# Setting the bulk elementwise work of neighbouring chunks between the two operations of a scan step

## The chip, the cores and the metric

The kernel runs on one core of a Trainium2 chip. The time is device time in microseconds (us) of one execution. A run more than 1.5% above the fastest of its kernel counts as slow. Medians below are of all runs, ratios of the fast runs alone. Comments in the cuts of code and of diffs are added here.

## The reference

A gated linear-attention layer is followed by a mixture of experts that sends each row to one expert. Only the attention part matters here, above all its decay `a`, whose modulus is cut at 0.999, and the running product over time.

```python
mag = np.sqrt(a_re * a_re + a_im * a_im)
scale = np.minimum(mag, 0.999) / (mag + 1e-06)
a_re_n, a_im_n = (a_re * scale, a_im * scale)
for t in range(S):                      # S = 768
    ar, ai = (a_re_n[:, :, t, :, None], a_im_n[:, :, t, :, None])
    new_re = ar * S_re - ai * S_im
    new_im = ar * S_im + ai * S_re
    ...                                 # kv, the product of k and v of this step
    S_re, S_im = (new_re + kv, new_im)
    y[:, :, t] = np.einsum('bhd,bhde->bhe', q[:, :, t], S_re)
```

## The kernel before

The sequence is cut into pieces of L = 96 steps. `elem(r)` treats half of all pieces (a round), one in each of 128 partitions. It runs a scan of complex products backwards over the 96 steps: each step is a multiply into `x` and an add into `A[:, t]`, and the add of one step feeds the multiply of the next. The round is worked in 12 chunks of T = 8 steps. Around the scan stands bulk work on whole chunks: the modulus stage, which makes the normalised `a` (`an`), and the stage that turns the finished scan into scaled q (`Qh`) and k. Then `units(r)` does the matmuls of the round. The program order is `elem(0)`, `units(0)`, `elem(1)`, `units(1)`, experts. A scheduler places the instructions of all stages into the queues of the engines, so part of `elem(1)` runs beside `units(0)`.

```python
st = ctx.enter_context(tc.tile_pool(name="st", bufs=2))
...
def elem(r):
    A = qt.tile([P, L + 1, 2, D], F32, name="A")
    QT = qt.tile([C, P, L], F32, name="QT")          # one buffer each
    ...
    for c in range(L // T - 1, -1, -1):
        t0 = c * T
        ...                                           # load ab
        sq = st.tile([P, 2, T, D], F32, name="sq")
        nc.scalar.activation(sq[:], ab[:], Act.Square)
        m = st.tile([P, T, D], F32, name="m", bufs=3)
        nc.vector.tensor_tensor(m[:], sq[:, 0], sq[:, 1], Alu.add)
        ...                                           # Ln, Exp, Copy on ScalarE: m, g
        nc.vector.scalar_tensor_tensor(g[:], m[:], 1.0, g[:], Alu.min, Alu.mult)
        an = st.tile([P, T, 4, D], F32, name="an")
        nc.vector.tensor_tensor(an[...], ab[:], planes(g, T), Alu.mult)
        ...                                           # two copies of an on ScalarE
        for t in range(t0 + T - 1, t0 - 1, -1):       # the scan
            x = st.tile([P, 2, 2, D], F32, name="x")
            nc.vector.tensor_tensor(x[:], A[:, t + 1, ...], an[:, t - t0]..., Alu.mult)
            nc.vector.tensor_tensor(A[:, t], x[:, 0], x[:, 1], Alu.add)
        ...                                           # load qc, kc
        e = A[:, t0 + 1:t0 + T + 1]
        sq = st.tile([P, T, 2, D], F32, name="sqe", tag="sq")      # shares the ring of sq
        nc.scalar.activation(sq[:], e, Act.Square)
        m = st.tile([P, T, D], F32, name="me", tag="m", bufs=3)    # shares the ring of m
        nc.vector.tensor_tensor(m[:], sq[:, :, 0], sq[:, :, 1], Alu.add)
        ...                                           # Ln, Exp on ScalarE
        nc.vector.tensor_tensor(qc[:], qc[:], m[:], Alu.mult)
        nc.vector.tensor_tensor(Qh[:], e, qc..., Alu.mult)
        nc.vector.tensor_tensor(e, e, kc..., Alu.mult)
        ...                                           # store e, transpose Qh on PE, copy to QT
```

Of the kernel before, what the change touches and what calls it, by code (L numbers as in the profile page):

```python
# [10 lines left out]
F32 = mybir.dt.float32  # L11
BF16 = mybir.dt.bfloat16
AX = mybir.AxisListType
Alu = mybir.AluOpType
Act = mybir.ActivationFunctionType
# [7 lines left out]
def gate_loop(nc, ctx, tc, cpool, ident, identb, q, k, v, a_re, a_im, wgp, x_rows, lg):  # L23


    B, H, S, D = q.shape
    L = 96
    G = S // L
    P = 128
# [3 lines left out]
    C = 2 * D  # L33
    T = 8

    qt = ctx.enter_context(tc.tile_pool(name="qt", bufs=1))
    st = ctx.enter_context(tc.tile_pool(name="st", bufs=2))
    un = ctx.enter_context(tc.tile_pool(name="un", bufs=2))
    ps = ctx.enter_context(tc.psum_pool(name="aps", bufs=1))

    kh = nc.dram_tensor("kh", (NR, P, L, C), F32, kind="Internal").ap()
# [6 lines left out]
    def rows(x, r):  # L48
        return x[r * NB:(r + 1) * NB].rearrange("b h (g t) d -> (b h g) t d", t=L)

    def planes(x, n):
        return x[:, None].broadcast_to([P, 2, n, D])

    for_round = []

    def elem(r):
        A = qt.tile([P, L + 1, 2, D], F32, name="A")
        QT = qt.tile([C, P, L], F32, name="QT")
        for_round.append(QT)
        nc.vector.memset(A[:, L, 0, :], 1.0)  # L60
        nc.vector.memset(A[:, L, 1, :], 0.0)
        for c in range(L // T - 1, -1, -1):
            t0 = c * T
            ab = st.tile([P, 2, T, D], F32, name="ab")
            nc.sync.dma_start(out=ab[:, 0], in_=rows(a_re, r)[:, t0:t0 + T])
            nc.sync.dma_start(out=ab[:, 1], in_=rows(a_im, r)[:, t0:t0 + T])
            sq = st.tile([P, 2, T, D], F32, name="sq")
            nc.scalar.activation(sq[:], ab[:], Act.Square)
            m = st.tile([P, T, D], F32, name="m", bufs=3)
            nc.vector.tensor_tensor(m[:], sq[:, 0], sq[:, 1], Alu.add)  # L70

            nc.scalar.activation(m[:], m[:], Act.Ln, scale=1.0 / (0.999 * 0.999))
            nc.scalar.activation(m[:], m[:], Act.Exp, scale=-0.5)
            g = st.tile([P, T, D], F32, name="g")
            nc.scalar.activation(g[:], m[:], Act.Copy, scale=-1e-6 / 0.999, bias=1.0)  # L75
            nc.vector.scalar_tensor_tensor(g[:], m[:], 1.0, g[:], Alu.min, Alu.mult)

            an = st.tile([P, T, 4, D], F32, name="an")
            nc.vector.tensor_tensor(an[:, :, 0:2, :].rearrange("p t c d -> p c t d"), ab[:], planes(g, T), Alu.mult)
            nc.scalar.activation(an[:, :, 2, :], an[:, :, 1, :], Act.Copy, scale=-1.0)  # L80
            nc.scalar.activation(an[:, :, 3, :], an[:, :, 0, :], Act.Copy)  # L81
            for t in range(t0 + T - 1, t0 - 1, -1):
                x = st.tile([P, 2, 2, D], F32, name="x")
                nc.vector.tensor_tensor(x[:], A[:, t + 1, :, None, :].broadcast_to([P, 2, 2, D]), an[:, t - t0].rearrange("p (u w) d -> p u w d", u=2), Alu.mult)  # L84
                nc.vector.tensor_tensor(A[:, t], x[:, 0], x[:, 1], Alu.add)  # L85

            qc = st.tile([P, T, D], F32, name="qc")
            kc = st.tile([P, T, D], F32, name="kc")
            nc.sync.dma_start(out=qc[:], in_=rows(q, r)[:, t0:t0 + T])
            nc.sync.dma_start(out=kc[:], in_=rows(k, r)[:, t0:t0 + T])  # L90
            e = A[:, t0 + 1:t0 + T + 1]
            sq = st.tile([P, T, 2, D], F32, name="sqe", tag="sq")
            nc.scalar.activation(sq[:], e, Act.Square)  # L93
            m = st.tile([P, T, D], F32, name="me", tag="m", bufs=3)
            nc.vector.tensor_tensor(m[:], sq[:, :, 0], sq[:, :, 1], Alu.add)
            nc.scalar.activation(m[:], m[:], Act.Ln)
            nc.scalar.activation(m[:], m[:], Act.Exp, scale=-1.0)
            nc.vector.tensor_tensor(qc[:], qc[:], m[:], Alu.mult)
            Qh = st.tile([P, T, 2, D], F32, name="Qh")
            nc.vector.tensor_tensor(Qh[:], e, qc[:, :, None, :].broadcast_to([P, T, 2, D]), Alu.mult)  # L100
            nc.vector.tensor_tensor(e, e, kc[:, :, None, :].broadcast_to([P, T, 2, D]), Alu.mult)
            nc.sync.dma_start(out=kh[r, :, t0:t0 + T], in_=e.rearrange("p t c d -> p t (c d)"))
            for t4 in range(0, T, 4):
                tp = ps.tile([C, 4, P], F32, name="tq", tag="tp", bufs=2)
                for i in range(4):
                    nc.tensor.transpose(tp[:, i, :], Qh[:, t4 + i].rearrange("p c d -> p (c d)"), ident[:])  # L106
                nc.scalar.copy(QT[:, :, t0 + t4:t0 + t4 + 4], tp.rearrange("c t p -> c p t"))
        nc.sync.dma_start(out=c_scr[r], in_=A[:, 0].rearrange("p c d -> p (c d)"))

    def units(r):  # L110
# [77 lines left out]

    nc.scalar.preload_act_table_set("natural_log_exp_and_others")
    elem(0)  # L190
    for r in range(NR):
        units(r)
        if r + 1 < NR:
            elem(r + 1)
# [184 lines left out]
def kernel(  # L379
# [34 lines left out]
    with ExitStack() as gstack:  # L414
        gate_loop(nc, gstack, tc, cpool, ident, identb, q, k, v, a_re, a_im, wgp, x_rows, lg)
# [31 lines left out]
```

## Time and profile before

| | before |
|---|---|
| median of the runs | 916.6 us at first; 909.96 us of the four runs that stand against the changed kernel |
| first scan stage, from the first multiply to the last bulk multiply | 147.7 us |
| first units stage, to its last mask multiply | 153.3 us |
| the rest of `elem(1)`, with no matmuls of units beside it ("scan alone") | 100.9 us |
| second units stage, to the first weight load | 155.3 us |
| the rest: weights and experts | 351.2 us |

A stage is read from the start times in the timeline of VectorE. In a timeline line stand the start, the duration, the engine, the source line, the operation, out and in, and in brackets the idle time just before it and what ended it. In the kernel before, the square of the finished chunk (L93) comes first, and the square of the next chunk's `a` (L68) only behind it, although its input was there long before (the loads were issued at 10.6 and 10.9 us, and no load of `ab` took over 5.3 us):

```profile
28.73 0.84 ACT L93 ACTIVATE sqe<-A 128x768 f32<-128x768 f32 x1 [4.82 <-DVE A L85]
29.48 0.83 ACT L68 ACTIVATE sq<-ab 128x768 f32<-128x768 f32 x1
...
35.44 0.52 ACT L80 ACTIVATE an<-an 128x384 f32<-128x384 f32 x1
35.87 0.51 ACT L81 ACTIVATE an<-an 128x384 f32<-128x384 f32 x1
```

ScalarE sat idle for 4.82 us before L93, while VectorE ran the scan, and the L68 behind it, which was ready, did not pass it. The copies L80 and L81, for which the next scan waits, end only at 36.38 us. VectorE kept its order in the same way: the scan multiply at 215.71 us (0.34 us) had its result at 216.05, but the add that reads it started only at 216.97, behind a `state` operation (L169) for which the engine sat idle for 0.65 us until 216.69.

### The profile page before, as it was taken

The numbers are of one execution on the slowest core, as the hardware profiler recorded it, in microseconds if no ns is written. First come the engines' busy times: TensorE is split into PE (matmuls) and PEld (weight loads), VectorE is DVE, ScalarE is ACT, GpSimd is POOL, SyncE is SP. The second block draws the span as 40 slices with busy tenths as digits, with TensorE's granted clock in tenths as the row PEclk, the third lists the DMA queues.
The fourth block names the chain that finished last, engine by engine and source line by source line (L and its number), as shares of the span: only waits on it lengthen the run. The fifth ranks groups of instructions, "written<-read, shape, count | busy, mean of one in ns | idle before, by whom it ended". The sixth has DMA issues, their size and how long they took to land. (4 is left out here: it accounts for less than half of the span.)

```text
span 919.8 us, 11601 instructions
## 1 busy us (share of the span) xinstructions
PE 586.6 (64%) x3599; PEld 373.8 (41%) x3599; DVE 375.7 (41%) x835; ACT 281.5 (31%) x620; POOL 82.6 (9%) x122
## 2 busy tenths in 40 slices
PE   0111111798899811117999995008999999999996
PEld 0011111566667611115667774006444444444443
DVE  5777777127657777770243331160111111111100
ACT  4444454134545745532233432000111111111111
POOL 0000000000000000000000002212222121221201
PEclk9999999997868965555578968555656666665657
DMA  4233333424543243214233313996010110101100
GB/s 120 88 103 103 103 97 87 100 66 99 134 115 85 65 155 103 80 34 101 66 88 78 88 44 44 207 208 123 26 40 31 35 39 27 40 28 38 23 1 1
DMA packets 104774, 71.58 MB, mean 78 GB/s; under 512 B 72878, under 2 KB 96930, under 8 KB 104720
## 3 DMA queue, kind: packets, MB, share of 16 engines
q0 software_dynamic: 14992, 20.36, 10.9%
q1 hardware_dynamic: 24768, 30.82, 10.8%
q10 hardware_dynamic: 64960, 19.67, 9.7%
q8 instruction: 35, 0.57, 0.3%
q14 instruction: 19, 0.16, 0.1%
HBM read 66.79 MB, written 17.99 MB: 92 GB/s over the span
## 5 line engine op out<-in xcount | busy, mean ns | idle before, releaser
L364 PE MATMUL h_ps<-xgT,w1s 128*128 128x128 bf16 x744 | 169.1, 248 | 20.6 <-DVE xgT L357 14.6
L106 PE MATMUL tq<-ident,Qh 128*96 128x128 f32 x192 | 41.8, 391 | 215.7 <-DVE Qh L100 214.0
L364 PEld LDWEIGHTS <-w1s 128*128 x744 | 76.1, 102 | 118.0 <-issue 42.3
L106 PEld LDWEIGHTS tq<-ident,Qh 128*96 128x96 f32 x192 | 31.6, 181 | 225.1 <-ACT g L75 176.9
L369 ACT ACTIVATE hT<-h_ps 128x512 bf16<-128x512 f32 x31 | 18.5, 597 | 235.8 <-PE h_ps L364 235.8
L160 PE MATMUL py<-KW,V 96*64 96x192 f32 x512 | 84.4, 414 | 5.1 <-issue 4.1
L146 DVE TENSOR_TENSOR KW<-wp,mask 96x384 f32<-96x384 f32 x64 | 35.2, 553 | 126.2 <-PE wp L145 125.3
L372 PE MATMUL y_ps<-w2s,hT 128*128 x248 | 82.9, 512 | 0.0
L84 DVE TENSOR_TENSOR x<-A,an 128x192 f32<-128x192 f32 x192 | 68.6, 357 | 31.1 <-ACT an L81 25.4
L145 PE MATMUL wp<-QT,KT 96*96 96x96 f32 x512 | 74.9, 314 | 1.5 <-ACT KT L140 1.4
L357 DVE COPY xgT<-xg_ps 128x384 bf16<-128x384 bf16 x31 | 11.1, 358 | 149.5 <-PE xg_ps L355 149.5
L145 PEld LDWEIGHTS wp<-QT,KT 96*96 96x96 f32 x512 | 66.5, 220 | 11.7 <-ACT Zs L152 4.9
L367 DVE TENSOR_SCALAR hT<-h_ps 128x512 bf16<-128x512 f32 x31 | 21.4, 691 | 92.2 <-PE h_ps L364 92.2
L133 POOL MEMSET V<- 96x128 f32 x32 | 6.4, 201 | 531.8 <-PE py L160 531.8
L85 DVE TENSOR_TENSOR A<-x 128x96 f32<-128x96 f32 x192 | 49.4, 257 | 6.4
L164 PE MATMUL py<-QT,Zs 96*48 96x96 f32 x448 | 49.0, 286 | 0.0
L93 ACT ACTIVATE sqe<-A 128x768 f32<-128x768 f32 x24 | 20.2, 843 | 94.0 <-DVE A L85 94.0
L139 PE MATMUL tk<-ident,KW 96*96 96x96 f32 x256 | 40.6, 302 | 12.6 <-DMA KW<-kh 11.2
L160 PEld LDWEIGHTS py<-KW,V 96*64 96x64 f32 x512 | 41.4, 171 | 17.3 <-issue 12.6
L351 POOL DMA_INDIRECT xg<-x_rows,idg x31 | 30.2, 973 | 203.3 <-PE xg_ps L355 171.4
L372 PEld LDWEIGHTS <-hT 128*128 128x128 bf16 x248 | 35.3, 148 | 31.6 <-issue 30.8
L173 PE MATMUL lg_ps<-yT,wgp 128*8 128x96 f32 x256 | 38.4, 283 | 4.4 <-ACT yT L170 3.2
(115 smaller groups left out, 741.2 us busy)
## 6 DMA issues: line engine op xcount, KB each, us to landing
kh<-A SPq DMA_DIRECT2D x24, 384.0 KB, 2.6
KW<-kh ACTq DMA_DIRECT2D x32, 288.0 KB, 3.1
w1s<-in_moe_w_dram POOLq DMA_DIRECT2D x8, 768.0 KB, 27.6
w2s<-in_moe_w_dram POOLq DMA_DIRECT2D x8, 768.0 KB
cB<-c_scr ACTq DMA_DIRECT2D x28, 192.0 KB, 3.9
ab<-in_a_re_dram SPq DMA_DIRECT2D x24, 192.0 KB, 3.0
V<-in_v_dram ACTq DMA_DIRECT2D x32, 144.0 KB, 2.8
ab<-in_a_im_dram SPq DMA_DIRECT2D x24, 192.0 KB, 3.3
```

The source lines that it names most:

```text
L84: nc.vector.tensor_tensor(x[:], A[:, t + 1, :, None, :].broadcast_to([P, 2, 2, D]), an[:, t - t0].rearrange("p (u w) d -> p u w d", u=2), ...
L85: nc.vector.tensor_tensor(A[:, t], x[:, 0], x[:, 1], Alu.add)
L106: nc.tensor.transpose(tp[:, i, :], Qh[:, t4 + i].rearrange("p c d -> p (c d)"), ident[:])
L139: nc.tensor.transpose(tp[:, i, :], KW[:, h4 + i, 0:C], ident[:L, :L])
L145: nc.tensor.matmul(wp[:, i, :], KT[:, h4 + i, :], QT[:, p, :], start=True, stop=True)
L146: nc.vector.tensor_tensor(KW[:, h4:h4 + 4, C:], wp[:], mask[:, None, :].broadcast_to([L, 4, L]), Alu.mult)
L160: nc.tensor.matmul(py[u * 64:(u + 1) * 64, i, :], V[:, 2 * j + u, :], KW[:, 2 * j + u, :], start=True, stop=(g == 0))
L164: nc.tensor.matmul(py[u * 64:u * 64 + D, i, C:], Zs[:, j, u * 64:u * 64 + D], QT[:, p, :], start=False, stop=True)
L173: nc.tensor.matmul(lg_ps[:, b, :], wgp[:, j, :], yT[:, j, :], start=(j == 0), stop=(j == J - 1))
L351: nc.gpsimd.indirect_dma_start(out=xg[:], out_offset=None, in_=x_rows_dram, in_offset=bass.IndirectOffsetOnAxis(ap=idg[:, i:i + 1], axis=0))
L364: nc.tensor.matmul(h_ps[:, f, :], w1s[:, bass.ds(te, 1), k, ff * 128:(ff + 1) * 128], xgT[:, k, :], start=(k == 0), stop=(k == KD - 1))
L372: nc.tensor.matmul(y_ps[:], hT[:, f, :], w2s[:, bass.ds(te, 1), f, :], start=(f == 0), stop=(f == NF - 1))
```

## The change

The intent: VectorE should not wait for ScalarE between two chunks, and the gaps between the dependent operations of the scan should be filled with work that does not depend on them. The modulus stage (`norm`) starts two chunks ahead, the q and k stage (`hats`) runs one chunk behind, and pieces of both are set between the multiply and the add of the scan steps. The normalised `a` gets a third buffer.

```diff
+    def norm(r, c, box):        # the modulus stage of one chunk, as before, with a
+        ...                     # yield ahead of each operation on VectorE
+        an = st.tile([P, T, 4, D], F32, name="an", bufs=3)
+    def hats(r, c, A, QT):      # the q and k stage of one chunk, likewise
+        ...
+        box = {}
+        last = L // T - 1
+        for c in (last, last - 1):
+            for _ in norm(r, c, box):
+                pass
+        for c in range(last, -2, -1):
+            hs = hats(r, c + 1, A, QT) if c < last else iter(())
+            ns = norm(r, c - 2, box) if c > 1 else iter(())
+            beside = [ns, hs, ns, hs, hs, ns, hs, hs, ns]
+            next(ns, None)
+            next(hs, None)
+            if c >= 0:
+                an = box.pop(c)
+                for t in range(c * T + T - 1, c * T - 1, -1):
                     nc.vector.tensor_tensor(x[:], ...)
+                    if beside:
+                        next(beside.pop(0), None)
                     nc.vector.tensor_tensor(A[:, t], x[:, 0], x[:, 1], Alu.add)
+            for g in (ns, hs):
+                for _ in g:
+                    pass
```

More of the change, by code (lines that the diff above doesn't have):

```diff
@@ L54, in gate_loop @@
     for_round = []
+    def norm(r, c, box):
+        t0 = c * T
+        ab = st.tile([P, 2, T, D], F32, name="ab")
+        nc.sync.dma_start(out=ab[:, 0], in_=rows(a_re, r)[:, t0:t0 + T])
+        nc.sync.dma_start(out=ab[:, 1], in_=rows(a_im, r)[:, t0:t0 + T])
+        sq = st.tile([P, 2, T, D], F32, name="sq")
+        nc.scalar.activation(sq[:], ab[:], Act.Square)
+        yield
+        m = st.tile([P, T, D], F32, name="m", bufs=3)
+        nc.vector.tensor_tensor(m[:], sq[:, 0], sq[:, 1], Alu.add)
+        nc.scalar.activation(m[:], m[:], Act.Ln, scale=1.0 / (0.999 * 0.999))
+        nc.scalar.activation(m[:], m[:], Act.Exp, scale=-0.5)
+        g = st.tile([P, T, D], F32, name="g")
+        nc.scalar.activation(g[:], m[:], Act.Copy, scale=-1e-6 / 0.999, bias=1.0)
+        yield
+        nc.vector.scalar_tensor_tensor(g[:], m[:], 1.0, g[:], Alu.min, Alu.mult)
+        yield
+        an = st.tile([P, T, 4, D], F32, name="an", bufs=3)
+        nc.vector.tensor_tensor(an[:, :, 0:2, :].rearrange("p t c d -> p c t d"), ab[:], planes(g, T), Alu.mult)
+        nc.scalar.activation(an[:, :, 2, :], an[:, :, 1, :], Act.Copy, scale=-1.0)
+        nc.scalar.activation(an[:, :, 3, :], an[:, :, 0, :], Act.Copy)
+        box[c] = an
@@ new lines, in hats @@
+    def hats(r, c, A, QT):
+        t0 = c * T
+        qc = st.tile([P, T, D], F32, name="qc")
+        kc = st.tile([P, T, D], F32, name="kc")
+        nc.sync.dma_start(out=qc[:], in_=rows(q, r)[:, t0:t0 + T])
+        nc.sync.dma_start(out=kc[:], in_=rows(k, r)[:, t0:t0 + T])
+        e = A[:, t0 + 1:t0 + T + 1]
+        sq = st.tile([P, T, 2, D], F32, name="sqe", tag="sq")
+        nc.scalar.activation(sq[:], e, Act.Square)
+        yield
+        m = st.tile([P, T, D], F32, name="me", tag="m", bufs=3)
+        nc.vector.tensor_tensor(m[:], sq[:, :, 0], sq[:, :, 1], Alu.add)
+        nc.scalar.activation(m[:], m[:], Act.Ln)
+        nc.scalar.activation(m[:], m[:], Act.Exp, scale=-1.0)
+        yield
+        nc.vector.tensor_tensor(qc[:], qc[:], m[:], Alu.mult)
+        yield
+        Qh = st.tile([P, T, 2, D], F32, name="Qh")
+        nc.vector.tensor_tensor(Qh[:], e, qc[:, :, None, :].broadcast_to([P, T, 2, D]), Alu.mult)
+        yield
+        nc.vector.tensor_tensor(e, e, kc[:, :, None, :].broadcast_to([P, T, 2, D]), Alu.mult)
+        nc.sync.dma_start(out=kh[r, :, t0:t0 + T], in_=e.rearrange("p t c d -> p t (c d)"))
+        for t4 in range(0, T, 4):
+            tp = ps.tile([C, 4, P], F32, name="tq", tag="tp", bufs=2)
+            for i in range(4):
+                nc.tensor.transpose(tp[:, i, :], Qh[:, t4 + i].rearrange("p c d -> p (c d)"), ident[:])
+            nc.scalar.copy(QT[:, :, t0 + t4:t0 + t4 + 4], tp.rearrange("c t p -> c p t"))
@@ L61, in elem @@
         nc.vector.memset(A[:, L, 1, :], 0.0)
-        for c in range(L // T - 1, -1, -1):
-            t0 = c * T
-            ab = st.tile([P, 2, T, D], F32, name="ab")
-            nc.sync.dma_start(out=ab[:, 0], in_=rows(a_re, r)[:, t0:t0 + T])
-            nc.sync.dma_start(out=ab[:, 1], in_=rows(a_im, r)[:, t0:t0 + T])
-            sq = st.tile([P, 2, T, D], F32, name="sq")
-            nc.scalar.activation(sq[:], ab[:], Act.Square)
-            m = st.tile([P, T, D], F32, name="m", bufs=3)
-            nc.vector.tensor_tensor(m[:], sq[:, 0], sq[:, 1], Alu.add)
-            nc.scalar.activation(m[:], m[:], Act.Ln, scale=1.0 / (0.999 * 0.999))
-            nc.scalar.activation(m[:], m[:], Act.Exp, scale=-0.5)
-            g = st.tile([P, T, D], F32, name="g")
-            nc.scalar.activation(g[:], m[:], Act.Copy, scale=-1e-6 / 0.999, bias=1.0)
-            nc.vector.scalar_tensor_tensor(g[:], m[:], 1.0, g[:], Alu.min, Alu.mult)
-            an = st.tile([P, T, 4, D], F32, name="an")
-            nc.vector.tensor_tensor(an[:, :, 0:2, :].rearrange("p t c d -> p c t d"), ab[:], planes(g, T), Alu.mult)
-            nc.scalar.activation(an[:, :, 2, :], an[:, :, 1, :], Act.Copy, scale=-1.0)
-            nc.scalar.activation(an[:, :, 3, :], an[:, :, 0, :], Act.Copy)
-            for t in range(t0 + T - 1, t0 - 1, -1):
-                x = st.tile([P, 2, 2, D], F32, name="x")
-                nc.vector.tensor_tensor(x[:], A[:, t + 1, :, None, :].broadcast_to([P, 2, 2, D]), an[:, t - t0].rearrange("p (u w) d -> p u w d", u=2), Alu.mult)
-                nc.vector.tensor_tensor(A[:, t], x[:, 0], x[:, 1], Alu.add)
-            qc = st.tile([P, T, D], F32, name="qc")
-            kc = st.tile([P, T, D], F32, name="kc")
-            nc.sync.dma_start(out=qc[:], in_=rows(q, r)[:, t0:t0 + T])
-            nc.sync.dma_start(out=kc[:], in_=rows(k, r)[:, t0:t0 + T])
-            e = A[:, t0 + 1:t0 + T + 1]
-            sq = st.tile([P, T, 2, D], F32, name="sqe", tag="sq")
-            nc.scalar.activation(sq[:], e, Act.Square)
-            m = st.tile([P, T, D], F32, name="me", tag="m", bufs=3)
-            nc.vector.tensor_tensor(m[:], sq[:, :, 0], sq[:, :, 1], Alu.add)
-            nc.scalar.activation(m[:], m[:], Act.Ln)
-            nc.scalar.activation(m[:], m[:], Act.Exp, scale=-1.0)
-            nc.vector.tensor_tensor(qc[:], qc[:], m[:], Alu.mult)
-            Qh = st.tile([P, T, 2, D], F32, name="Qh")
-            nc.vector.tensor_tensor(Qh[:], e, qc[:, :, None, :].broadcast_to([P, T, 2, D]), Alu.mult)
-            nc.vector.tensor_tensor(e, e, kc[:, :, None, :].broadcast_to([P, T, 2, D]), Alu.mult)
-            nc.sync.dma_start(out=kh[r, :, t0:t0 + T], in_=e.rearrange("p t c d -> p t (c d)"))
-            for t4 in range(0, T, 4):
-                tp = ps.tile([C, 4, P], F32, name="tq", tag="tp", bufs=2)
-                for i in range(4):
-                    nc.tensor.transpose(tp[:, i, :], Qh[:, t4 + i].rearrange("p c d -> p (c d)"), ident[:])
-                nc.scalar.copy(QT[:, :, t0 + t4:t0 + t4 + 4], tp.rearrange("c t p -> c p t"))
@@ new lines, in elem @@
+        box = {}
[12 more added lines that the diff above has]
+                for t in range(c * T + T - 1, c * T - 1, -1):
+                    x = st.tile([P, 2, 2, D], F32, name="x")
+                    nc.vector.tensor_tensor(x[:], A[:, t + 1, :, None, :].broadcast_to([P, 2, 2, D]), an[:, t - c * T].rearrange("p (u w) d -> p u w d", u=2), Alu.mult)
+                    if beside:
+                        next(beside.pop(0), None)
+                    nc.vector.tensor_tensor(A[:, t], x[:, 0], x[:, 1], Alu.add)
+            for g in (ns, hs):
+                for _ in g:
+                    pass
```

## The prediction

> **What bounds the kernel now.** I read the busy tenths of the page first, to split the span into stages.
>
> ```profile
> PE   0111111798899811117999995008999999999996
> ...
> DVE  5777777127657777770243331160111111111100
> ACT  4444454134545745532233432000111111111111
> ...
> PEclk9999999997868965555578968555656666665657
> ```
>
> A slice is 23 us. In slices 0 to 6 and 14 to 17 PE is idle and VectorE leads: this is the scan stage alone, first `elem(0)`, then the part of `elem(1)` that did not fit beside `units(0)`. Slices 7 to 13 are `units(0)` with the rest of `elem(1)`, 18 to 23 `units(1)`, then weight loads and the experts. Next, the timeline of VectorE gives the borders: `elem(0)` scans from 11.48 to 159.2 us, and the last mask multiply of `units(0)` and the first of `units(1)` are
>
> ```profile
> 312.46 0.55 DVE L146 TENSOR_TENSOR KW<-wp,mask 96x384 f32<-96x384 f32 x1 [0.82 <-PE wp L145]
> ...
> 422.72 0.55 DVE L146 TENSOR_TENSOR KW<-wp,mask 96x384 f32<-96x384 f32 x1 [9.40 <-PE wp L145]
> ```
>
> so about 148 us and 101 us (312.5 to 413.3, where the last L101 ends) are scan stage alone. One chunk of it on VectorE, from the end of one scan to the start of the next (start, duration, then the idle time before it and who ended it):
>
> ```profile
> 29.13 0.26 DVE L85 TENSOR_TENSOR A<-x 128x96 f32<-128x96 f32 x1
> 29.61 0.56 DVE L95 TENSOR_TENSOR me<-sqe 128x384 f32<-128x384 f32 x1 [0.23 <-ACT sqe L93]
> 30.34 0.56 DVE L70 TENSOR_TENSOR m<-sq 128x384 f32<-128x384 f32 x1 [0.17 <-ACT sq L68]
> 31.31 0.56 DVE L98 TENSOR_TENSOR qc<-qc,me 128x384 f32<-128x384 f32 x1 [0.41 <-ACT me L97]
> 31.91 0.96 DVE L100 TENSOR_TENSOR Qh<-A,qc 128x768 f32<-128x768 f32 x1
> 32.84 0.56 DVE L76 SCALAR_TENSOR_TENSOR g<-m,g 128x384 f32<-128x384 f32 x1
> 33.31 0.95 DVE L101 TENSOR_TENSOR A<-A,kc 128x768 f32<-128x768 f32 x1
> 34.18 0.95 DVE L79 TENSOR_TENSOR an<-ab,g 128x768 f32<-128x768 f32 x1
> 36.41 0.36 DVE L84 TENSOR_TENSOR x<-A,an 128x192 f32<-128x192 f32 x1 [1.28 <-ACT an L81]
> ```
>
> Two things are to be seen. VectorE waits on ScalarE four times per chunk (0.23 + 0.17 + 0.41 + 1.28 = 2.09 us). And a start-to-start interval depends on who is next: L76 to L101, independent, 0.47 us for a 0.56 us operation; L101 to L79 0.87 us for 0.95 us; but L84 to L85, where the second reads the first, 0.39 us for 0.36, and L85 to the next L84 0.29 us for 0.26. The scan is made of such dependent pairs:
>
> ```profile
> L84 DVE TENSOR_TENSOR x<-A,an 128x192 f32<-128x192 f32 x192 | 68.6, 357 | 31.1 <-ACT an L81 25.4
> L85 DVE TENSOR_TENSOR A<-x 128x96 f32<-128x96 f32 x192 | 49.4, 257 | 6.4
> ```
>
> A step is 0.39 + 0.29 = 0.68 us. An independent operation starts about 0.085 us before its predecessor ends and a dependent one 0.03 us after, so an operation set between a pair hides about 0.115 us. One chunk takes 12.47 us (23.94 to 36.41).
>
> The units stage is led by PE, at two speeds:
>
> ```profile
> 200.56 1.49 PE L145 MATMUL wp<-QT,KT 96*96 96x96 f32 x8
> 203.68 0.92 PE L145 MATMUL wp<-QT,KT 96*96 96x96 f32 x8
> ```
>
> eight of the same matmuls in 1.49 and in 0.92 us. The change adds no PE work.
>
> [...]
>
> **The change, part by part.** It removes no operation. The bulk operations, W, are per chunk four small (m, me, qc, g; 0.47 us each when hidden) and three large (an, Qh, multiply by kc; 0.87 us each): 4 x 0.47 + 3 x 0.87 = 4.49 us. I compared the queue orders of the built kernels. The steady chunk becomes: an, x, me, A, m, x, A, qc, x, Qh, A, multiply by kc, x, g, A, then four bare steps. So the scheduler puts some W after A rather than between x and A; the gain is the same. All seven W sit in separate gaps, and the modulus stage runs far enough ahead that the 1.28 us wait for L81 cannot recur.
>
> Chunk after: 8 x 0.684 + 4.49 - 7 x 0.115 = 9.15 us. The waits: me and m find their squares ready, since the last scan result that the square needs comes one step before the chunk's end. For qc I lay out ScalarE's new queue order (sqe, sq, two an copies, then Ln and Exp of me): an ends 0.96 us into the chunk, the copies (0.52 us each, starts 0.43 apart) keep ScalarE to 1.93, Ln and Exp to 2.98, qc wants 2.82: 0.2 us. So about 9.35 us, 3.1 less than now.
>
> `elem(0)`: two modulus stages come before the first x. Its ScalarE and VectorE work delays it by about 1.6 us, to 13.1. After that 96 x 0.684 = 65.7; ten modulus sets at 1.81 = 18.1; twelve of the others at 2.68 = 32.2; two early m of `elem(1)` 0.9; minus 73 filled gaps in the new order x 0.115 = 8.4: 108.5. Waits 11 x 0.2 = 2.2, and about 2 for the last me to qc, which has nothing beside it. End at 125.8 instead of 159.2: **33.4 us saved**.
>
> Scan alone after `units(0)`: the new order leaves 58 steps (64 before), 27 small and 26 large W, 42 filled gaps: 39.7 + 12.7 + 22.6 - 4.8 = 70.2, waits and end 3.5, so 73.7 against 100.9: **27 us saved**.
>
> Inside `units(0)` (153 us from the end of `elem(0)` to its last mask multiply) VectorE gets six more steps and a few W, by intervals 36.3 to 41.0 us. The queue is in order and was 77% busy at the end of this stage, so I charge nearly all: **4 us lost**. `units(1)`, weights and experts: no change. Sum: -33.4 - 27 + 4 = -56.4 on 916.6, **860 us**.
>
> **Rivals.**
> (1) ScalarE's chain takes the place of the wait: me to qc or Ln/Exp queue behind QT copies or squares, and an in-order VectorE then stops the scan. Against it: ScalarE is busy some 45% of the stage now, so about 60% of a 9.35 us chunk. For it: each W has one fixed place. Another 1 us per chunk over some 19 chunks makes 879.
> (2) Loads or the PE stage become the bound. Loads and stores per chunk stay 4 x 192 + 384 KB, 126 GB/s at the new pace against 92 over the span, while slices 25 and 26 moved over 200 GB/s, and the buffers free two chunks ahead: unlikely. But `units(0)` may stretch, since the scan's operations are placed among its mask multiplies by a schedule, not by the chip[...]. That could return 10 to 15 us (872), or save as much (848).
> (3) Only dependency gaps are gained and the waits come back elsewhere: about 20 chunks x 7 x 0.115 = 16 us, 900. The queue order speaks against it, as the wait for an is gone by construction.
>
> **Range and chances.** The two scan-only savings are sums of measured intervals; I give them +-6 us together. `units(0)` and the clock give +-12, and the before runs alone spread over 903 to 920. So 843 to 878. A change below 2% (over 898) needs rival 3 nearly whole: faster 0.96, same 0.03, slower 0.01.
>
> **What would show it.** VectorE busy time stays about 376 us. The wait of the scan for the an copies (25.4 us at L84) falls to near zero; chunk period 9.1 to 9.6 us in 30 to 110 us; the last `elem(0)` multiply ends at 123 to 129 us; scan alone between the units takes 71 to 77 us. If the chunk period is over 10 us the ScalarE step failed; if the stages fit and the total doesn't, `units(0)` or the clock did it.

## The result and the profile after

The changed kernel took 853.75 us (median of four runs, 849.14 to 855.97), the kernel before 909.96 us (902.92 to 919.84). The ratio is 0.9447, with a 95% interval of 0.9378 to 0.9515. A ratio here is the mean time of one kernel's fast runs over that of the other's of the same rounds, so it is not the ratio of the medians: 0.9447 is 853.2 / 903.1, and two of the four runs of the kernel before (916.62 and 919.84) count as slow. Fast against fast the gain is 50.0 us; the medians differ by 56.2.

The busy tenths of the changed kernel, 21 us to a slice:

```profile
PE   0122128998889712299998930179999999999996
...
DVE  5999971256767999523334320700111101111110
ACT  6766542253645874333434310001111111111111
...
PEclk9999999967977955567879975555665656566665
```

VectorE now fills its slices in the first scan stage (9 where there were 7), and that stage ends inside slice 5, not 6. The two scan groups:

```profile
L132 DVE TENSOR_TENSOR x<-A,an 128x192 f32<-128x192 f32 x192 | 68.2, 355 | 6.1 <-ACT an L78 1.8
...
L135 DVE TENSOR_TENSOR A<-x 128x96 f32<-128x96 f32 x192 | 49.1, 255 | 4.4
```

The durations are the same. The idle time for the copies of `an` fell from 25.4 to 1.8 us. One steady chunk of the changed kernel in the timeline of VectorE:

```profile
48.46 0.95 DVE L76 TENSOR_TENSOR an<-ab,g 128x768 f32<-128x768 f32 x1
49.33 0.35 DVE L132 TENSOR_TENSOR x<-A,an 128x192 f32<-128x192 f32 x1
49.60 0.55 DVE L93 TENSOR_TENSOR me<-sqe 128x384 f32<-128x384 f32 x1
50.07 0.25 DVE L135 TENSOR_TENSOR A<-x 128x96 f32<-128x96 f32 x1
50.23 0.55 DVE L66 TENSOR_TENSOR m<-sq 128x384 f32<-128x384 f32 x1
50.70 0.35 DVE L132 TENSOR_TENSOR x<-A,an 128x192 f32<-128x192 f32 x1
51.09 0.26 DVE L135 TENSOR_TENSOR A<-x 128x96 f32<-128x96 f32 x1
51.38 0.56 DVE L97 TENSOR_TENSOR qc<-qc,me 128x384 f32<-128x384 f32 x1
51.86 0.35 DVE L132 TENSOR_TENSOR x<-A,an 128x192 f32<-128x192 f32 x1
52.13 0.95 DVE L100 TENSOR_TENSOR Qh<-A,qc 128x768 f32<-128x768 f32 x1
53.00 0.25 DVE L135 TENSOR_TENSOR A<-x 128x96 f32<-128x96 f32 x1
...
57.69 0.95 DVE L76 TENSOR_TENSOR an<-ab,g 128x768 f32<-128x768 f32 x1
```

A chunk takes 9.23 us, 48.46 to 57.69, against 12.47 (12.53 in the later chunks of the kernel before). No line has a bracket. A bulk operation starts 0.27 us after a multiply of 0.35 us, and the add behind it 0.47 us later. One small stall is left: `qc` starts 0.29 us after the add at 51.09, not 0.17 as a bulk operation does after the adds at 50.07 and 53.00, since Exp on ScalarE ends at 51.35. On ScalarE the squares and copies now stand well ahead:

```profile
47.89 0.84 ACT L90 ACTIVATE sqe<-A 128x768 f32<-128x768 f32 x1 [1.35 <-DVE A L135]
48.64 0.83 ACT L63 ACTIVATE sq<-ab 128x768 f32<-128x768 f32 x1
49.45 0.52 ACT L77 ACTIVATE an<-an 128x384 f32<-128x384 f32 x1
49.88 0.51 ACT L78 ACTIVATE an<-an 128x384 f32<-128x384 f32 x1
```

These copies belong to a chunk whose scan starts two chunks later, at 67.78 us, so nobody waits for them. The borders of the stages with no matmuls of units:

```profile
281.69 0.55 DVE L177 TENSOR_TENSOR KW<-wp,mask 96x384 f32<-96x384 f32 x1
...
363.79 0.55 DVE L177 TENSOR_TENSOR KW<-wp,mask 96x384 f32<-96x384 f32 x1 [9.42 <-PE wp L176]
```

Between these two, scan alone ends at 354.4 us: 72.7 us in place of 100.9. The table has the stages of all traces, in us, with the mean granted PE clock of the two units stages in brackets. "First scan" holds some work of the second round in e4, e5 and e9.

| trace | first scan | first units | scan alone | second units | rest |
|---|---|---|---|---|---|
| before | 147.7 | 153.3 (0.87) | 100.9 | 155.3 (0.74) | 351.2 |
| before, e7 | 147.7 | 150.2 (0.93) | 100.9 | 149.1 (0.77) | 351.9 |
| changed | 111.3 | 158.0 (0.85) | 72.7 | 144.7 (0.82) | 352.1 |
| changed, e8 | 111.3 | 144.0 (0.86) | 72.6 | 155.7 (0.74) | 351.2 |
| e1_lump | 120.8 | 149.4 (0.89) | 85.6 | 140.1 (0.84) | 352.1 |
| e2_ahead | 111.2 | 143.9 (0.86) | 71.3 | 154.2 (0.74) | 352.0 |
| e3_between | 111.0 | 155.3 (0.87) | 75.7 | 144.4 (0.82) | 352.0 |
| e4_rings | 115.2 | 167.2 (0.81) | 56.9 | 147.4 (0.80) | 352.0 |
| e5_early | 115.3 | 165.2 (0.78) | 47.9 | 145.0 (0.81) | 350.8 |
| e6_tiny | 120.8 | 151.9 (0.88) | 85.6 | 147.3 (0.79) | 351.8 |
| e9, early again | 115.2 | 158.7 (0.82) | 47.9 | 138.0 (0.86) | 351.1 |

The two scan stages repeat to 0.1 us between traces of one kernel, the rest to 0.9 us. The units stages do not. The clocks of the first units stage are not to be relied on, as e7 and e8 show below.

### The profile page after: what moved, and what is told of

The parts are those of the page before. It is cut to its first block, busy times and chain, and to the rows that moved or that the text cites. A ratio compares the mean times of both kernels' runs of the same rounds, so it can differ in the third digit from the quotient of the medians.

```text
span 851.2 us, 11577 instructions
## 1 busy us (share of the span) xinstructions
PE 581.7 (68%) x3599; PEld 367.9 (43%) x3599; DVE 360.2 (42%) x835; ACT 280.2 (33%) x620; POOL 82.8 (10%) x122
## 5 line engine op out<-in xcount | busy, mean ns | idle before, releaser
L191 PE MATMUL py<-KW,V 96*64 96x192 f32 x512 | 82.3, 405 | 7.4 <-issue 7.3
L177 DVE TENSOR_TENSOR KW<-wp,mask 96x384 f32<-96x384 f32 x64 | 35.3, 553 | 120.3 <-PE wp L176 119.2
L176 PE MATMUL wp<-QT,KT 96*96 96x96 f32 x512 | 72.0, 305 | 2.1 <-ACT KT L171 1.9
L132 DVE TENSOR_TENSOR x<-A,an 128x192 f32<-128x192 f32 x192 | 68.2, 355 | 6.1 <-ACT an L78 1.8
L176 PEld LDWEIGHTS wp<-QT,KT 96*96 96x96 f32 x512 | 64.0, 212 | 12.2 <-ACT KT L171 5.4
L191 PEld LDWEIGHTS py<-KW,V 96*64 96x64 f32 x512 | 39.5, 167 | 18.5 <-issue 15.1
L108 ACT COPY QT<-tq 96x512 f32<-96x512 f32 x48 | 27.5, 583 | 47.0 <-PE tq L107 44.0
L201 ACT COPY yT<-py 128x192 f32<-128x192 f32 x64 | 20.5, 320 | 65.9 <-DVE state L200 60.9
## 6 DMA issues: line engine op xcount, KB each, us to landing
V<-in_v_dram ACTq DMA_DIRECT2D x32, 144.0 KB, 2.9
```

What stands on the lines that cost most here:

```text
L108: nc.scalar.copy(QT[:, :, t0 + t4:t0 + t4 + 4], tp.rearrange("c t p -> c p t"))
L132: nc.vector.tensor_tensor(x[:], A[:, t + 1, :, None, :].broadcast_to([P, 2, 2, D]), an[:, t - c * T].rearrange("p (u w) d -> p u w d", u=2 ...
L176: nc.tensor.matmul(wp[:, i, :], KT[:, h4 + i, :], QT[:, p, :], start=True, stop=True)
L177: nc.vector.tensor_tensor(KW[:, h4:h4 + 4, C:], wp[:], mask[:, None, :].broadcast_to([L, 4, L]), Alu.mult)
L191: nc.tensor.matmul(py[u * 64:(u + 1) * 64, i, :], V[:, 2 * j + u, :], KW[:, 2 * j + u, :], start=True, stop=(g == 0))
```

## The experiments

All kernels gave correct results. e1 to e4 ran on one chip, e5 to e7 on a second and e8 and e9 on a third, each group with its own runs of the kernel before. The profiled runs of e3 and e4 were slow. Of these, mainly the scan stages are used, which do not show that: the first scan is 115.2 us in e4 and 115.3 us in the fast trace of e5, and 111.0 us in e3 against 111.2 in the fast trace of e2. Where their units stages are used, the text says so.

### e1_lump: no waits, but no filled gaps either

```diff
-            ns = norm(r, c - 2, box) if c > 1 else iter(())
-            beside = [ns, hs, ns, hs, hs, ns, hs, hs, ns]
+            ns = norm(r, c - 3, box) if c > 2 else iter(())
...
-                    if beside:
-                        next(beside.pop(0), None)
...
+            for g in (older_h, older_n, older_h, older_n, older_h, hs, ns):
+                next(g, None)            # one block behind the eight steps
+            older_n, older_h = ns, hs    # Ln and Exp of a stage run under the next scan
```

Each of these operations of VectorE is also tied to the one before it by an edge that fixes the order and waits for nothing.

> The changed kernel with the same operations, but the eight scan steps of a chunk run bare and the seven bulk operations stand in one block behind them, each bulk stage one chunk further ahead so that VectorE need not wait for ScalarE; the queue order on VectorE is fixed by ordering edges without a wait. It takes the hidden gaps away and keeps the waits away. Theory A (both count: 2.5 us per chunk of waits and about 0.7 us of gaps): a steady chunk takes 9.85 us against 9.22 in the changed kernel, the scan of the first round ends near 132 us against 123.7, and the whole takes about 866 us. Theory B (only the waits count, setting between is worth nothing): chunk 9.2 us, 854 us. Theory C (only the gaps count): chunk over 11.6 us, about 897 us.

Measured: 868.58 us (ratio to before 0.9475, interval 0.9378 to 0.9571). A steady chunk of this kernel, with the seven bulk operations in the left-out lines:

```profile
49.94 0.35 DVE L141 TENSOR_TENSOR x<-A,an 128x192 f32<-128x192 f32 x1
50.32 0.26 DVE L142 TENSOR_TENSOR A<-x 128x96 f32<-128x96 f32 x1
50.61 0.36 DVE L141 TENSOR_TENSOR x<-A,an 128x192 f32<-128x192 f32 x1
...
59.77 0.35 DVE L141 TENSOR_TENSOR x<-A,an 128x192 f32<-128x192 f32 x1
```

The chunk takes 9.83 us (49.94 to 59.77), which theory A had at 9.85. So of the 3.24 us that a chunk lost, 2.64 go with the waits for ScalarE (12.47 to 9.83) and 0.60 are gaps filled (9.83 to 9.23). Of the 2.64, 2.09 are the idle time in the brackets of the old chunk. The other 0.55 are, by an estimate from its start-to-start intervals, overlaps of neighbours that the waits and the dependent pair L98 and L100 had prevented. Theories B and C fall. The first scan took 9.4 us longer than in the changed kernel, scan alone 12.9 us longer. Part of the latter is not gaps: the waits of VectorE there hold 5.2 us once for the transposes of the held-back `Qh`, and twice 2.2 us for Exp at the end. The expected end of the first scan, 132 us, was missed: it came at 136.0, as the scan also began 2.8 us later (15.22 against 12.39).

### e2_ahead: the list beside the steps emptied

```diff
-            beside = [ns, hs, ns, hs, hs, ns, hs, hs, ns]
+            beside = []
```

> The changed kernel with its list of what goes beside a scan step empty: in the program the bulk operations stand behind the eight steps. The modulus stage stays two chunks ahead. Theory A (the scheduler, not the place in the program, sets the queue order; the built order of this kernel is nearly that of the changed one, 74 filled gaps in the first round against 73): chunk 9.2 us, scan of the first round ends near 124 us, 852 us. Theory B (the place in the program matters): bare steps, chunk 9.9 us, about 866 us.

Measured: 848.45 us (ratio 0.9254, interval 0.916 to 0.9348), first scan 111.2 us, scan alone 71.3 us. Its timeline has the bulk work between the steps all the same:

```profile
48.41 0.95 DVE L76 TENSOR_TENSOR an<-ab,g 128x768 f32<-128x768 f32 x1
49.28 0.35 DVE L132 TENSOR_TENSOR x<-A,an 128x192 f32<-128x192 f32 x1
49.55 0.55 DVE L93 TENSOR_TENSOR me<-sqe 128x384 f32<-128x384 f32 x1
50.02 0.25 DVE L135 TENSOR_TENSOR A<-x 128x96 f32<-128x96 f32 x1
```

Theory A holds. Where the program puts these operations makes no difference; the scheduler fills a gap as soon as it has something ready for it. Gaps filled are worth 0.60 us per chunk, but the line that was written to fill them is not what fills them.

### e3_between: one chunk ahead in place of two

```diff
-        an = st.tile([P, T, 4, D], F32, name="an", bufs=3)
+        an = st.tile([P, T, 4, D], F32, name="an")
...
-        for c in (last, last - 1):
+        for c in (last,):
...
-            ns = norm(r, c - 2, box) if c > 1 else iter(())
+            ns = norm(r, c - 1, box) if c > 0 else iter(())
```

> The changed kernel with the modulus stage one chunk ahead in place of two, and two buffers for the normalised a. Theory A (any run-ahead past the scan is enough, as the built queue order is the same in the steady chunk): chunk 9.2 us, stage alone after the first units round 75.5 us against 72.7, 855 us. Theory B (two chunks are needed): the wait of the scan for the copies of the normalised a comes back, 1.28 us in each chunk, chunk about 10.4 us, 877 us.

Measured: 849.75 us (ratio 0.913, interval 0.903 to 0.923); a chunk 9.22 us, first scan 111.0 us, scan alone 75.7 us. All its scan waited 0.9 us for the copies. Theory A holds: one chunk ahead and two buffers are enough. The 3 us more of scan alone fit the order in the traces, which leaves two more steps there (60 against 58) and one more modulus stage (7 `an` against 6). And as `an` is back at two buffers, this kernel has the same buffers as the kernel before: no additional buffer was needed.

### e4_rings: the kernel before, with rings of their own

If neither the place in the program nor the second chunk ahead matters, what had held the modulus stage back? In the kernel before, the squares of both stages share one ring of two buffers, and the magnitudes one of three. I took the ring to hand out its buffers in program order, so that the square of the next chunk's `a` had to come behind the square of this chunk's scan. This test changes nothing else:

```diff
-            m = st.tile([P, T, D], F32, name="m", bufs=3)
+            m = st.tile([P, T, D], F32, name="m")
...
-            sq = st.tile([P, T, 2, D], F32, name="sqe", tag="sq")
+            sq = st.tile([P, T, 2, D], F32, name="sqe")
...
-            m = st.tile([P, T, D], F32, name="me", tag="m", bufs=3)
+            m = st.tile([P, T, D], F32, name="me")
```

> The kernel before, with one thing changed: the squares and the magnitudes of the two bulk stages no longer share their rings of buffers (own rings of two each). Nothing is moved in the program. Theory A (what kept the modulus stage from running ahead was the shared ring, which hands out buffers in program order, so the next chunk's squares had to come after this chunk's; the built queue order now has 74 filled gaps in the first round): nearly the whole gain without the change, chunk 9.2 to 9.5 us, stage alone after the first units round about 57 us since only 39 scan steps are left there, against 72.7; 13 early steps of the second round delay the first mask multiply by 5 to 9 us; about 846 us. Theory B (the moved program order is what counts): waits stay at 2.1 us per chunk, chunk 12.5 us, 910 us.

Measured: 846.59 us (ratio 0.9166, interval 0.9064 to 0.9269), a chunk 9.24 us, scan alone 56.9 us; the first mask multiply came at 140.8 us, 7.8 us later than in the changed kernel. Every number of theory A was met. On ScalarE the square of a later chunk's `a` (L68) now runs in the midst of the scan, 4.4 us ahead of the square of the finished chunk (L93), and the scan groups of VectorE show that the wait is gone:

```profile
51.84 0.84 ACT L68 ACTIVATE sq<-ab 128x768 f32<-128x768 f32 x1 [1.03 <-DMA ab<-in_a_im_dram]
...
56.25 0.84 ACT L93 ACTIVATE sqe<-A 128x768 f32<-128x768 f32 x1
...
L84 DVE TENSOR_TENSOR x<-A,an 128x192 f32<-128x192 f32 x192 | 68.1, 355 | 5.4 <-ACT an L81 1.0
```

So three edited lines give the whole gain of the change. It costs 7.5 KB per partition for buffers (worked out from the tile shapes), where the change costs 6. What the moved program does is to take the buffers of the shared rings in another order. That this order was the cause of the 2.64 us rests on two runs: e3 keeps the shared rings and every buffer count and only moves the program, e4 keeps the program and splits the rings, and either ends the wait. Which of the two rings held the stage back (squares or magnitudes), and whether more buffers in a shared ring would do as well, was not tested.

### e5_early: more of the second round beside the first units stage

With own rings, the scan of `elem(1)` no longer waits for its q and k stage. That stage cannot finish before `units(0)`, as `QT` has one buffer. So its twelve sets were moved behind the scan, and the scan was emitted six steps at a time.

```diff
-        units(r)
-        if r + 1 < NR:
-            elem(r + 1)
+        es = elem(r + 1, late=True) if r + 1 < NR else iter(())
+        for _ in units(r):               # yields after each of 16 pieces
+            for _ in range(6):
+                next(es, None)           # one scan step
+        for _ in es:                     # late: the q and k stage of all chunks
+            pass
```

> The kernel before with own rings as in the run e4_rings, and the second round's scan and modulus stage emitted six steps after each of the sixteen pieces of the first units round, so that only the twelve sets of the other bulk operations (magnitude, q and k products) are left after it: in the built order 6 scan steps there against 39 in e4_rings and 58 in the changed kernel. The stage alone after the first units round should take about 40 us (56.9 in e4_rings, 72.7 in the changed kernel). Inside the first units round VectorE gets 19 us more of such work by summed intervals. Theory A (VectorE's idle time there, some 75 of 158 us, takes in half or more): that stage 167 to 177 us, the whole about 838 us. Theory B (the queue in order charges all of it to the matmuls): that stage 186 us, the whole about 848 us, no gain over e4_rings.

Measured: 829.24 us (ratio 0.9143, interval 0.9041 to 0.9245). Scan alone fell to 47.9 us, not to 40. The waits of VectorE in that stage say why:

```profile
DVE qc L69 <- ACT me L68: 9.1, 5, 2.1
DVE KW L156 <- PE wp L155: 1.6, 1, 1.6
DVE A L72 <- DMA kc<-in_k_dram: 0.9, 1, 0.9
```

With no scan left to hide it, the chain of magnitude, Ln and Exp on ScalarE is waited for again, 9.1 us in all. The first units stage took 165.2 us here, and 158.7 in the second trace (e9), against 167.2 in the slow run of e4; theory A had 167 to 177. But these lengths move with the speed of the matmuls (see e7 and e8). What is left of the stage after PE's busy time does not: it is 19.7 us in both traces of the changed kernel, 22.9 in e4, and 28.6 and 30.6 in the two traces of this kernel. So of 16.8 us more busy time of VectorE there (95.4 in e4, 112.2 here), 6 to 8 us went to PE's idle time: the larger part was hidden, as theory A says, but not all.

### e6_tiny: an instruction more in every gap

```diff
                     keep(nc.vector.tensor_tensor(x[:], ...))
+                    keep(nc.vector.memset(tiny[:], 0.0))
                     keep(nc.vector.tensor_tensor(A[:, t], x[:, 0], x[:, 1], Alu.add))
```

> The kernel of e1_lump (bare steps in fixed order) with one more VectorE instruction, a memset of a 128x48 tile that nobody reads, in each of the 192 gaps between the two operations of a scan step. Two of the setup memsets of that size stand 0.06 us apart. Theory A (the 0.39 us between the two operations is the first one's latency with an open slot of about 0.12 us in it): a step stays 0.68 us and a steady chunk stays 9.83 us, the whole stays at about 865 us. Theory B (0.39 us is what the engine needs per instruction, and each further one adds its own interval): a step takes 0.74 us or more, the chunk 10.3 us, the whole about 11.5 us longer.

Measured (one run): 874.74 us. The added instruction in the trace:

```profile
51.02 0.36 DVE L142 TENSOR_TENSOR x<-A,an 128x192 f32<-128x192 f32 x1
51.33 0.10 DVE L143 MEMSET tiny<- 128x48 f32 x1
51.41 0.26 DVE L144 TENSOR_TENSOR A<-x 128x96 f32<-128x96 f32 x1
51.70 0.36 DVE L142 TENSOR_TENSOR x<-A,an 128x192 f32<-128x192 f32 x1
```

A step stays 0.68 us (51.02 to 51.70), and both scan stages stay at 120.8 and 85.6 us, to the tenth as in e1, with 152 instructions more. Theory A holds: the gap is an open slot. The total missed its expected 865: this trace spans 9.9 us more than that of e1, and 9.7 of them lie in the two units stages. In the second (7.2 us) there are no memsets; in the first (2.5 us) there are 40 of the 192, so there a small cost is not excluded.

### e7_before_again and e8_after_again: how far the units stages move by themselves

Both kernels once more, unchanged.

> The kernel before, unchanged, for a second trace. If the 10.6 us by which the second units round was shorter in the changed kernel's trace (144.7 against 155.3 us) come from the granted clock and not from the change, then this trace again shows the two scan-only stages at 147.7 and 100.9 us within 0.5 us, while its two units rounds move by 5 us or more from 153.3 and 155.3 us. If the change shortened the second units round, they stay within 2 us.

> The changed kernel, unchanged, on the same chip as e9_early_again and with a second trace. Theory A (the units stages move with the granted clock): the two scan-only stages again take 111.3 and 72.7 us within 0.5 us, while the first units round moves by several us from the 158.0 us of the first trace, since the nearly identical queue of e2_ahead took 143.9 us there; the 4.7 us by which it was longer than in the kernel before would then be within the scatter. Theory B (the 4 us that the prediction charged are real): 157 to 159 us again. The whole about 850 us.

Measured: 913.55 us (one run) and 853.94 us (ratio to before 0.9418, interval 0.9281 to 0.9555). The two scan stages repeat to 0.1 us. The second units stage moved by 6.2 us between the two traces of the kernel before, and by 11.0 us between the two of the changed kernel; the first moved by 3.1 and 14.0 us. The e7 trace alone met its test for one of its two stages only (3.1 us is less than the 5 I asked for), so the other traces decide. In the windows of the changed kernel's two traces, the two lines are the first and the second units stage; the columns are busy time of PE, PE weight loads, VectorE, ScalarE and GpSimd, then granted PE clock, DMA share and GB/s. First trace:

```profile
123.71:281.69 157.98, 138.33 (x1088) 103.09 (x1085) 83.52 (x189) 72.73 (x191) 3.03 (x15) 0.85 0.38 95
...
354.37:499.07 144.70, 127.57 (x1133) 96.31 (x1131) 46.64 (x89) 52.10 (x148) 2.63 (x13) 0.82 0.32 76
```

Second trace:

```profile
123.73:267.74 144.01, 124.35 (x1087) 93.74 (x1085) 83.07 (x189) 72.60 (x191) 3.02 (x15) 0.86 0.41 104
340.38:496.11 155.73, 138.74 (x1133) 105.13 (x1131) 46.62 (x89) 52.18 (x148) 2.62 (x14) 0.74 0.30 70
```

In the second units stage VectorE and ScalarE do the same 46.6 and 52.1 us of work. PE runs the same 1133 matmuls, but they keep it busy for 127.57 and 138.74 us, and its clock differs. Over all eleven traces of the table (the slow ones of e3 and e4 too) this stage goes with its granted clock: 154.2 to 155.7 us at 0.74, 149.1 at 0.77, 147.3 at 0.79, 147.4 at 0.80, 145.0 at 0.81, 144.4 and 144.7 at 0.82, 140.1 at 0.84, 138.0 at 0.86. What is left after PE's busy time is 15.7 to 17.2 us in all of them. A nearly unchanged program (e2) got 0.74 as well.

The first units stage is the same story, though its mean clocks (0.85 and 0.86) hide it: PE was busy for 138.33 and 124.35 us there, and the difference is the whole 14.0 us. The trace lists the clock as 1.00 up to its first change (at some 174 and 148 us), but the matmuls before it were not fast. Eight of the `wp` matmuls took 1.49 us at 164.6 us and 0.92 only at 167.7 us in the first trace, while the second has 0.92 at 143.3 us already. At the start of the stage the slow rate lasted for some 35 us in one trace and for some 10 us in the other, and for some 37 us in the kernel before (eight of L145 in 1.49 us still at 200.6 us, in 0.92 at 203.7; PE was busy for 35.3 of the 37.6 us from 166.0 to 203.6). Later in the kernel before, eight of these took 1.60 us at 249.7 us, where the listed clock is 0.50. So the units stages move by the speed of the same matmuls, and their lengths give nearly all by which two traces of one kernel differ: 9.3 us against 8.0 us of span for the kernel before (919.8 and 911.8), 3.0 against 3.9 for the changed kernel (851.2 and 847.3), 13.5 against 13.1 for e5 and e9 (836.3 and 823.2). What sets it in a given run stays open.

### e9_early_again: against the changed kernel on one chip

> The kernel of e5_early, unchanged, for a comparison with the changed kernel on one chip. Expected near 830 us, 2 to 3 per cent under e8_after_again; if the first units round takes back what the shorter stage after it gains, the two differ by less than 1 per cent.

Measured: fast runs 824.92, 836.0 and 832.97 us, against 849.01, 861.57, 855.54 and 852.33 us of the changed kernel. The ratio of the means is 831.3 / 854.6 = 0.973. Two slow runs (842.31 and 840.1) are left out; with all five it is 0.977. The version of e5 beats both kernels, but part of this is the speed of the matmuls: scan alone is 24.8 us shorter, the first scan 4.0 longer, and PE is idle for 9 to 11 us more in the first units stage, which leaves 10 to 12 us (an estimate from the traces).

## Why the prediction was right

- **The bound.** Right. Both scan-only stages were set by VectorE (in the changed kernel busy for 86.3 of the 90 us from 20 to 110 us, where the kernel before had 70.8). They lost 36.4 us (147.7 to 111.3) and 28.2 us (100.9 to 72.7), and the weights and experts moved by under 1 us.
- **A chunk of 9.15 us by intervals, 9.35 with a wait for `qc`.** Measured 9.23. The wait is there, but 0.12 us in place of 0.2. e1 measured the two parts of the gain apart: 2.64 us that go with the waits and 0.60 us of gaps. e6 showed that the gap is an open slot, as the argument needed: with a memset of 0.10 us in it a step stayed 0.68 us.
- **The first scan stage, 33.4 us saved.** Measured 35.5 at its end (159.2 to 123.7). Two modulus stages ahead of the scan delayed its start by 0.9 us, not 1.6, and the small waits were shorter.
- **Scan alone, 27 us saved.** Measured 28.2; the queue order gave the 58 steps, and the sum of intervals held.
- **Inside `units(0)`, 4 us lost.** This step is not borne out. One trace shows +4.7 us, which looks like a hit, but a second trace of the same kernel shows 144.0 us. The means are 151.8 us before (153.3, 150.2) and 151.0 after (158.0, 144.0). Less PE's busy time, which moves with the speed of the matmuls, 19.3 and 22.0 us are left before and 19.7 in both traces after, although VectorE's busy time there rose from 78.6 to 83.5 us. So the step that failed is to charge added VectorE work in full to the matmuls: these 5 us were hidden, and in e5 more than half of 16.8.
- **VectorE's busy time stays about 376 us.** Wrong, it is 360.2. The groups' own sums are as before (68.6 and 68.2 us for the multiply), but busy time counts overlapping instructions once, and independent neighbours overlap by some 0.085 us. This had no part in the sum.
- **The total.** 860 us predicted, 853.75 measured. The medians differ by 56.2 us in the first set of runs, and by 61.1 us in that of e8 (915.08 and 853.94); fast runs alone, by the two ratios, by about 50 and 53. The two scan terms measured sum to -63.7. The kernel before itself went from 902 to 920 us in the first set, and two traces of it differ by the units stages, so that 56.2 falls on the 56.4 of the prediction is luck: two terms were too small, one did not show, and the runs spread by more than the difference.
- **The rivals.** ScalarE's chain did not take the place of the wait (its share is the 0.12 us). The DMA queues did not (from 30 to 110 us, and in scan alone, the waits of VectorE in the changed kernel list none for DMA). The third, that only gaps are gained, is refuted by e1.
- **What the prediction did not see** is why the modulus stage had not run ahead before. It credited the two chunks ahead and the places beside the steps. e2, e3 and e4 show that neither is needed: the order in which the program took the buffers of the shared rings held it back.

## What to carry to other kernels

Where a scheduler orders the queues, look for what keeps an instruction from being ready before you move it in the program: here two stages that shared one ring of buffers took turns in program order, and rings of their own were worth as much as a restructured loop. In the chain of dependent vector operations here, the time between two of them held an open slot (a memset of 0.10 us in it, 152 times in two stages, left them at 120.8 and 85.6 us), which independent work fills for less than its own duration (0.60 us gained by seven operations in a chunk, 0.09 us each); count it by start-to-start intervals and not by durations. Before you explain a few microseconds of a stage, trace the same kernel twice (one stage took 144.0 and 158.0 us here, a difference of 1.6% of the span), and take the busy time of the engine that leads it off the stage's length.
